# A fused attention and MLP kernel: the same instructions in newly searched orders, with the last stores planned at their traced lengths

## The chip, the cores and the metric

The kernel runs on one core of a Trainium2 chip. The metric is the device time of one execution in microseconds; lower is better. Engines are named as in the profile: PE (TensorE), DVE (VectorE), ACT (ScalarE), POOL (GpSimd) and SP (SyncE, which only issues DMAs here).

## The reference

Causal attention with 16 extra "beacon" keys that every query sees, over 8 batches x 8 heads, 576 queries and head size 64; then a gated MLP over the 4608 tokens.

```python
scores = scale * np.matmul(q, k_all.transpose(0, 1, 3, 2))   # k_all: beacon_k, then k
scores = np.where(causal, -1000000000.0, scores)
a = np.exp(scores - scores.max(-1, keepdims=True))
a /= a.sum(-1, keepdims=True) + 1e-09
attn = np.matmul(a, v_all)                                    # (8, 8, 576, 64)
x = attn.transpose(0, 2, 1, 3).reshape(4608, 512)
h = x @ w_in                                                  # (512, 2048)
g = h * (1.0 / (1.0 + np.exp(-1.702 * h)))
out = g @ w_out                                               # (2048, 512)
```

## The kernel before

**Attention.** The 64 pairs of batch and head form 16 sets of four heads. The scores of a set are made transposed, keys on the partitions, in chunks of up to 512 columns a head (`e_qk`, matmuls at L559 and L570). ACT takes the exponential (L582), POOL sets the masked part of each block to zero (`affine_select`, L600), and from the fifth set on DVE adds up the key blocks for the softmax's denominators ("zs", `e_zadd`, L618). Products with v and with ones follow (`e_av`, L658), then transposes and a reciprocal on DVE (L668 to L679), and the normalized values go to `xT` (L696).

**MLP.** The tokens are cut into ten groups: two of 256 and eight of 512. Groups 2 to 9 compute the second matmul by seven products of a Strassen-like scheme (`products`, `e_prod`, L838): DVE first forms sums of quarters of g (`e_s`, L786, called "sums" below: 128x512 elements each, four a sum), PE multiplies, and DVE joins the products into the output tiles (`e_join`, L854). The first matmul of groups 3 to 9 is partly done the same way (`fast`, L925, with sums of the weights "SF" and of the tokens "sig"), and partly plainly (L720). A store of a 256x256 quarter of the output is one DMA of 256 KB issued by SP (`e_store4`, L862).

**The last group.** Its products come as 1, 2, 6, 7, 5, 4, 3. The quarters of the output lie in tiles "a" (product 2), "b" (product 5), "u" (product 4) and "m" (product 3). Products 5 and 3 share two accumulators, one for each half of 128 rows, so that the first half of "m" is stored on its own as 128 KB and the second half in two pieces of 64 KB, one on SP and one on ACT (`e_store2`, L869).

**What sets the order.** `Plan.op` records each piece of work with an engine, a planned duration in ns and what it depends on; "Q" is a planned DMA queue that issues nothing. `Plan.run` (its body is printed below) does not choose an order: it takes each engine's list from the table `ORDER` and the PSUM bank of each accumulator from the table `BANK`. Both tables were written by a search outside the program. The planned durations settle only in which order the program's text is emitted, and so the waits are the dependences alone. DVE and POOL are planned as excluding each other for the operations named in `HELD` and for the masks. A planned duration is the search's belief, and not what the chip does: for one sum 336 ns, for a mask 190 + 0.9 ns for each element a partition.

Loads of v, q, k and the weights, and the staging copies of q and k ("qD", "kD") are DMAs that POOL issues (L458 to L502); SP issues transposing DMAs from the staged copies (L492), and stores. Each engine's list is worked off in order: an instruction that waits holds back all that stand behind it on that engine.

Of the kernel before, what the change touches and what calls it, by code (L numbers as in the profile page):

```python
# [18 lines left out]
        126, 136, 165, 162, 129, 235, 147, 150, 152, 168, 240, 171, 249, 131, 242, 174, 177, 245, 194, 200, 197,  # L19
        266, 203, 209, 206, 275, 256, 212, 215, 284, 277, 252, 254, 261, 287, 259, 280, 180, 225, 181, 226, 291,  # L20
        289, 416, 182, 187, 188, 419, 183, 189, 227, 422, 294, 296, 228, 190, 429, 304, 318, 308, 306, 322, 302,
        324, 330, 312, 316, 320, 314, 328, 332, 310, 326, 218, 342, 447, 438, 343, 219, 344, 220, 221, 450, 351,
        362, 372, 352, 345, 476, 363, 373, 353, 364, 367, 354, 374, 610, 368, 365, 375, 369, 486, 613, 441, 370,
        445, 443, 619, 491, 386, 493, 489, 638, 387, 388, 389, 503, 379, 640, 380, 381, 505, 507, 382, 525, 519,
        539, 509, 521, 523, 512, 511, 547, 527, 528, 515, 543, 531, 537, 541, 545, 535, 549, 559, 560, 561, 643,
        629, 562, 568, 584, 569, 570, 579, 580, 800, 589, 585, 581, 571, 590, 803, 582, 586, 587, 591, 652, 806,
        592, 636, 634, 632, 655, 814, 657, 659, 596, 597, 832, 598, 599, 665, 603, 604, 835, 605, 606, 669, 671,
        866, 673, 674, 667, 677, 687, 681, 697, 711, 685, 683, 707, 689, 690, 699, 703, 701, 693, 705, 709, 721,
        722, 723, 996, 823, 876, 730, 724, 731, 732, 733, 828, 999, 830, 881, 879, 826, 883, 1006, 741, 742,
        758, 746, 747, 743, 1025, 744, 751, 748, 759, 760, 1027, 749, 752, 889, 753, 754, 1030, 891, 765, 761,  # L30
        766, 767, 895, 905, 768, 893, 931, 909, 897, 907, 898, 911, 913, 914, 927, 901, 917, 929, 921, 925, 923,
        935, 933, 945, 1016, 1039, 1187, 954, 946, 947, 955, 956, 948, 965, 966, 1190, 957, 967, 968, 1019,
        1023, 1193, 1021, 1042, 1044, 1046, 1201, 970, 982, 975, 971, 976, 1219, 972, 1052, 973, 983, 977, 1222,
        978, 984, 985, 1056, 1054, 1253, 989, 990, 1061, 991, 992, 1058, 1060, 1068, 1092, 1074, 1070, 1072,
        1090, 1064, 1076, 1077, 1096, 1094, 1088, 1086, 1098, 1084, 1080, 1108, 1210, 1263, 1399, 1117, 1109,
        1110, 1111, 1118, 1119, 1120, 1217, 1402, 1215, 1266, 1268, 1270, 1213, 1409, 1128, 1133, 1134, 1129,
        1130, 1428, 1135, 1136, 1138, 1139, 1131, 1430, 1140, 1145, 1146, 1276, 1141, 1433, 1147, 1152, 1278,
        1148, 1153, 1154, 1292, 1155, 1280, 1282, 1294, 1298, 1285, 1284, 1296, 1419, 1308, 1288, 1324, 1300,
        1310, 1301, 1328, 1326, 1330, 1312, 1332, 1333, 1304, 1442, 1424, 1316, 1336, 1317, 1314, 1447, 1449,
        1422, 1426, 1445, 1320, 1357, 1348, 1349, 1455, 1471, 1350, 1358, 1351, 1459, 1457, 1473, 1385, 1461,  # L40
        1386, 1463, 1464, 1475, 1487, 1359, 1467, 1360, 1368, 1477, 1369, 1370, 1479, 1378, 1480, 1371, 1491,
        1493, 1489, 1373, 1374, 1387, 1375, 1503, 1483, 1376, 1495, 1388, 1379, 1380, 1381, 1496, 1527, 1505,
        1507, 1392, 1393, 1528, 1394, 1395, 1499, 1512, 1511, 1509, 1582, 1536, 1529, 1552, 1515, 1537, 1538,
        1584, 1598, 1530, 1586, 1553, 1600, 1602, 1539, 1620, 1590, 1554, 1547, 1548, 1549, 1550, 1555, 1606,
        1588, 1591, 1557, 1558, 1604, 1559, 1594, 1560, 1614, 1607, 1610, 1571, 1572, 1616, 1573, 1630, 1574,
        1618, 1636, 1634, 1564, 1623, 1622, 1565, 1566, 1638, 1626, 1567, 1639, 1642, 1678, 1663, 1632, 1664,
        1654, 1655, 1665, 1656, 1673, 1674, 1666, 1657, 1675, 1679, 1680, 1676, 1683, 1684, 1685, 1681, 1686,
        1687, 1691, 1692, 1693, 1697, 1694, 1698, 1701, 1702,
# [3 lines left out]
        172, 243, 175, 178, 246, 195, 198, 201, 267, 204, 207, 210, 276, 213, 216, 278, 281, 417, 420, 184, 423,  # L52
        229, 431, 191, 430, 305, 309, 303, 307, 331, 313, 317, 323, 315, 325, 329, 321, 319, 311, 333, 327, 448,
        222, 451, 477, 350, 478, 611, 614, 620, 621, 639, 504, 641, 506, 520, 508, 526, 510, 522, 524, 540, 548,
        514, 544, 516, 532, 534, 530, 518, 546, 542, 536, 538, 550, 644, 567, 801, 804, 807, 815, 816, 833, 666,
        836, 670, 672, 868, 867, 668, 682, 678, 676, 686, 684, 680, 712, 688, 698, 700, 696, 704, 692, 702, 694,
        708, 706, 710, 997, 729, 1000, 1008, 1007, 1026, 1028, 890, 1031, 892, 906, 894, 896, 910, 908, 912,
        904, 928, 920, 916, 900, 918, 932, 922, 902, 930, 924, 926, 936, 934, 1188, 953, 1191, 1194, 1203, 1202,
        1220, 1053, 1223, 1057, 1254, 1255, 1055, 1069, 1059, 1093, 1071, 1073, 1063, 1091, 1075, 1065, 1079,
        1097, 1083, 1095, 1089, 1067, 1087, 1099, 1085, 1081, 1400, 1116, 1403, 1410, 1411, 1429, 1431, 1277,  # L60
        1434, 1279, 1293, 1281, 1283, 1299, 1295, 1291, 1297, 1309, 1289, 1325, 1287, 1303, 1329, 1327, 1331,
        1311, 1307, 1313, 1335, 1305, 1339, 1315, 1337, 1319, 1321, 1456, 1472, 1323, 1460, 1458, 1356, 1462,
        1474, 1466, 1470, 1468, 1488, 1476, 1478, 1482, 1486, 1494, 1490, 1492, 1484, 1504, 1506, 1502, 1498,
        1508, 1500, 1510, 1583, 1516, 1514, 1518, 1585, 1599, 1587, 1535, 1621, 1601, 1603, 1589, 1605, 1597,
        1593, 1595, 1615, 1613, 1617, 1609, 1631, 1611, 1619, 1637, 1635, 1641, 1627, 1643, 1629, 1625, 1633,
        1645, 1662, 1706,
# [3 lines left out]
        232, 233, 127, 157, 128, 161, 130, 167, 164, 148, 149, 151, 153, 250, 263, 132, 170, 173, 264, 413, 176,  # L70
        265, 179, 196, 199, 426, 251, 202, 205, 208, 211, 257, 258, 214, 285, 253, 255, 217, 286, 260, 415, 262,
        414, 473, 288, 290, 292, 293, 427, 616, 428, 295, 297, 434, 435, 436, 495, 298, 334, 474, 338, 299, 496,
        475, 497, 437, 335, 336, 300, 346, 339, 439, 440, 337, 341, 347, 340, 301, 348, 355, 482, 618, 617, 483,
        349, 484, 485, 359, 366, 487, 488, 442, 357, 371, 376, 358, 444, 446, 356, 492, 494, 490, 499, 390, 500,
        501, 498, 502, 625, 383, 513, 529, 533, 626, 517, 552, 556, 627, 551, 555, 628, 563, 553, 554, 564, 630,
        557, 565, 558, 566, 648, 631, 573, 649, 650, 576, 651, 574, 583, 588, 575, 653, 654, 572, 637, 635, 656,
        633, 658, 660, 593, 661, 600, 662, 663, 664, 607, 675, 819, 872, 679, 713, 717, 695, 691, 873, 874, 820,
        715, 821, 822, 714, 719, 875, 718, 727, 824, 825, 725, 877, 726, 878, 829, 738, 716, 831, 882, 880, 734,
        827, 884, 736, 720, 728, 885, 1012, 735, 737, 886, 745, 750, 887, 755, 1013, 888, 1014, 769, 1035, 762,
        899, 1015, 903, 915, 919, 1036, 1037, 938, 1038, 937, 941, 939, 942, 940, 944, 1017, 943, 949, 1018,  # L80
        950, 1040, 952, 959, 951, 1041, 962, 969, 1020, 958, 1024, 1043, 1045, 960, 1047, 1022, 1048, 1049, 961,
        1050, 974, 979, 986, 1051, 1206, 993, 1207, 1062, 1208, 1259, 1078, 1082, 1066, 1260, 1261, 1100, 1104,
        1262, 1103, 1209, 1107, 1102, 1101, 1211, 1105, 1112, 1212, 1113, 1264, 1265, 1125, 1218, 1106, 1121,
        1122, 1216, 1114, 1267, 1214, 1271, 1272, 1115, 1415, 1123, 1273, 1274, 1275, 1124, 1269, 1132, 1416,
        1137, 1417, 1142, 1438, 1149, 1439, 1440, 1418, 1156, 1290, 1286, 1420, 1302, 1441, 1340, 1306, 1421,
        1334, 1443, 1338, 1444, 1341, 1425, 1345, 1318, 1448, 1423, 1450, 1446, 1322, 1427, 1451, 1343, 1344,
        1452, 1352, 1353, 1453, 1342, 1454, 1362, 1346, 1354, 1361, 1347, 1355, 1465, 1469, 1365, 1481, 1485,
        1372, 1364, 1377, 1382, 1497, 1501, 1520, 1363, 1389, 1524, 1532, 1396, 1519, 1523, 1521, 1531, 1525,
# [1471 lines left out]
```

## Time and profile before

| what | us |
| --- | --- |
| median of three runs | 323.74 |
| lowest and highest | 323.15, 324.75 |
| the profiled execution's own time | 323.49 |
| its span, first to last instruction | 321.8 |
| PE busy | 311.4 |
| DVE busy | 249.7 |
| ACT busy | 227.1 |
| POOL busy | 135.9 |

In the rows of stretches, the columns behind the stretch are its length, then for each engine the busy us and in brackets the number of instructions, then the granted PE clock, the DMA share and GB/s. A waits row reads: who waited, at which tile and line, for whom; us in total, times, longest. A timeline row has start, duration, engine, line, operation and tiles, the number of merged instructions, and in brackets the idle time before it and what ended it; "SPq" is SP issuing a DMA. A group's row has busy us and mean ns of one, then idle time before. Matmul durations contain the pipeline's depth, so those that follow each other overlap: the start of one to the start of the next is the rate.

### The profile page before, as it was taken

What the parts mean: (1) busy time and instruction counts of PE and PEld (TensorE: products, weight loads), DVE (VectorE), ACT (ScalarE), POOL (GpSimd) and SP (SyncE); (2) the same over time, 40 slices, a digit from 0 to 9 for tenths busy, and PEclk for the clock granted to TensorE, in tenths of its full rate; (3) what the DMA queues carried; (4) which work ended last, traced back from release to release, by engine and by line L of the source; (5) the groups of instructions that cost most, each with busy time, mean ns of one, the idle gap of its engine ahead of it and who ended that gap; (6) DMA issues with size and microseconds to landing.
All of it is one profiled execution on the core that took longest, in us unless ns stands there. A gap on an engine that the chain in (4) does not pass through costs nothing.

```text
span 321.8 us, 9162 instructions
## 1 busy us (share of the span) xinstructions
PE 311.4 (97%) x3899; PEld 227.7 (71%) x3899; DVE 249.7 (78%) x489; ACT 227.1 (71%) x297; POOL 135.9 (42%) x186
## 2 busy tenths in 40 slices
PE   6999999999989999999999999999999999999992
PEld 2567874545757767776787578757788888888882
DVE  4777988489899579868987796688997973966681
ACT  1678883777748887699677977997699675466710
POOL 8759658580867902583229803900650000000000
PEclk9999999999999999999999999999999999999997
DMA  7999999998799994699199995990081000300303
GB/s 120 178 203 201 138 182 186 119 195 55 74 113 152 156 89 52 92 170 189 12 139 103 201 68 111 129 154 0 7 125 48 2 3 0 115 17 2 129 4 130
DMA packets 112522, 33.49 MB, mean 104 GB/s; under 512 B 97505, under 2 KB 109921, under 8 KB 112481
## 3 DMA queue, kind: packets, MB, share of 16 engines
q0 software_dynamic: 83008, 18.55, 65.2%
q1 hardware_dynamic: 29264, 14.28, 18.5%
q8 instruction: 30, 0.49, 0.6%
q14 instruction: 12, 0.09, 0.1%
q10 hardware_dynamic: 208, 0.07, 0.1%
HBM read 37.22 MB, written 14.22 MB: 160 GB/s over the span
## 4 chain that ended last, share of the span: by engine, by line
PE 56%; ACT 1%; DVE 1%; issue 0%; DVEq 0%
PE u L838 24%; PE u L925 16%; PE u L720 6%; PE u L658 5%; PE s L559 4%; ACT E L582 1%; DVE osb L854 0%; DVE rz L679 0%; DVE g L786 0%; ACT u L935 0%; DVE xT L696 0%; DVE zt L668 0%; ACT kn L941 0%; DVE rc L674 0%; DVEq L1555 0%
## 5 line engine op out<-in xcount | busy, mean ns | idle before, releaser
L582 ACT ACTIVATE E<-s 128x2048 f16<-128x2048 f32 (+3 forms) x59 | 90.8, 1551 | 33.4 <-PE s L570 16.5
L600 POOL TENSOR_SCALAR_AFFINE_SELECT E<-E 128x512 f16<-128x512 f16 (+3 forms) x78 | 59.2, 872 | 96.3 <-ACT E L582 85.8
L838 PEld LDWEIGHTS <-g 128*128 128x128 f16 x768 | 72.9, 98 | 12.6 <-issue 1.1
L838 PE MATMUL u<-w,g 128*128 128x256 f16 x512 | 67.3, 273 | 0.0
L720 PE MATMUL u<-xT,w 128*128 128x512 f16 (+1 forms) x320 | 59.5, 337 | 0.0
L950 ACT ACTIVATE g<-u 128x512 f16<-128x512 f32 x80 | 45.3, 608 | 13.3 <-PE u L925 7.4
L854 DVE SCALAR_TENSOR_TENSOR osb<-u,osb 128x512 f32<-128x512 f32 (+2 forms) x51 | 33.2, 655 | 23.9 <-PE u L838 22.0
L720 PEld LDWEIGHTS <-w 128*128 128x128 f16 x320 | 30.5, 98 | 21.8 <-issue 0.7
L474 POOL DMA_DIRECT2D vb<-in_v_dram x32 | 35.2, 1136 | 5.0 <-PE u L658 5.0
L925 PEld LDWEIGHTS <-SF 128*128 128x128 f16 x320 | 31.0, 98 | 7.7 <-issue 0.9
L838 PE MATMUL u<-tB,g 128*128 128x256 f16 x256 | 35.2, 273 | 0.5 <-DVE g L786 0.5
L925 PE MATMUL u<-sig,SF 128*128 128x256 f16 x240 | 33.9, 273 | 0.6 <-DVE sig L786 0.2
L696 DVE TENSOR_TENSOR xT<-u,rz 128x352 f16<-128x352 f32 (+6 forms) x58 | 25.9, 478 | 7.0 <-PE u L658 6.6
L742 ACT ACTIVATE g<-u 128x512 f16<-128x512 f32 x48 | 26.6, 617 | 4.1 <-PE u L720 4.0
L658 PE MATMUL u<-E,vb 128*32 128x352 f16 (+8 forms) x928 | 28.0, 263 | 0.3 <-DVE xT L696 0.2
L786 DVE TENSOR_TENSOR g<-g 128x512 f16<-128x512 f16 x64 | 28.0, 449 | 0.3
L618 DVE TENSOR_TENSOR zs<-zs,E 128x1344 f16<-128x1344 f16 (+2 forms) x36 | 24.0, 671 | 3.6 <-POOL E L600 1.7
L935 ACT ACTIVATE u<-u 128x512 f32<-128x512 f32 x40 | 23.1, 590 | 5.0 <-PE u L925 2.9
L925 PEld LDWEIGHTS <-w 128*128 128x128 f16 x240 | 23.3, 98 | 3.1
L658 PEld LDWEIGHTS <-vb 128*32 128x32 f16 (+1 forms) x928 | 20.2, 96 | 7.4 <-issue 3.5
L925 PE MATMUL u<-xT,w 128*128 128x256 f16 x160 | 23.6, 273 | 0.0
L944 DVE TENSOR_TENSOR u<-u,qn 128x512 f32<-128x512 f32 x20 | 13.4, 692 | 7.1 <-ACT g L950 4.1
(72 smaller groups left out, 434.3 us busy)
## 6 DMA issues: line engine op xcount, KB each, us to landing
out_dram<-osb SPq DMA_DIRECT2D x35, 256.0 KB, 3.4
vb<-in_v_dram POOLq DMA_DIRECT2D x24, 128.0 KB, 6.3
kn<-in_k_dram POOLq DMA_DIRECT2D x8, 288.0 KB, 6.7
qn<-in_q_dram POOLq DMA_DIRECT2D x8, 288.0 KB, 7.0
qD<-in_q_dram POOLq DMA_DIRECT2D x8, 288.0 KB, 8.0
kD<-in_k_dram POOLq DMA_DIRECT2D x8, 288.0 KB, 7.0
w<-in_moe_w_in_dram POOLq DMA_DIRECT2D x8, 256.0 KB, 8.2
w<-in_moe_w_out_dram POOLq DMA_DIRECT2D x4, 512.0 KB, 8.9
```

Source lines behind the costliest of these rows:

```text
L474: nc.gpsimd.dma_start(out=t[0 : hi - lo, j, h0:h1, :], in_=v[b, h0:h1, lo:hi, :].rearrange("h n d -> n h d"),)
L582: nc.scalar.activation(out=Es[s][:, h0:h1, c0:c1], in_=sall[(i, p)][:, :, o : o + c1 - c0], func=AFT.Exp, scale=0.125,)
L600: nc.gpsimd.affine_select(out=blk, in_=blk, compare_op=ALU.is_ge, fill=0.0, base=off + (Nb if j == 0 else 0), pattern=[[0, Q], [1, w]], ch ...
L658: nc.tensor.matmul(u[32 * h : 32 * h + 32, a:e], lhs, src[0:kw, h, col : col + e - a], start=first, stop=last, skip_group_check=s >= EARLY ...
L696: nc.vector.tensor_tensor(out=xT[:, 2 * hs + x : 2 * hs + x + n, at : at + c1 - c0], in0=rings[("av", s, x, half)][:, 0 : n * w].rearrange ...
L720: nc.tensor.matmul(u[:, o + a - t0 : o + e - t0], w1t[:, kp, nt * P : (nt + 1) * P], xT[:, kp, a % XR : (e - 1) % XR + 1], start=(kp == 0 ...
L742: nc.scalar.activation(out=gts[g][:, n0:n1, 0:w], in_=rings[("m1", g, n0)][:, 0 : n * w].rearrange("p (n w) -> p n w", n=n), func=AFT.Gelu ...
L786: (nc.vector if eng == "DVE" else nc.gpsimd).tensor_tensor(out=out, in0=a, in1=b, op=op)
L838: nc.tensor.matmul(u[:, HM * mt : HM * (mt + 1)], lhs[:, n, mt * P : (mt + 1) * P], rhs[:, n, :], start=(n == 0 and (mt == 0 or apart) and ...
L854: nc.vector.scalar_tensor_tensor(out=osbs[(g, dst)][:, c0:c1], in0=rings[("p", g, p)][:, c0:c1], scalar=scale_of(g), in1=osbs[(g, src)][:, ...
L925: nc.tensor.matmul(u[:, HM * n : HM * (n + 1)], lhs[x][:, (2 * i + n) * P : (2 * i + n + 1) * P], rhs[:, x, :], start=fresh and n == 0 and ...
L950: nc.scalar.activation(out=gts[g][:, n : n + 2, HM * h : HM * (h + 1)], in_=rings[src][:, :].rearrange("p (n w) -> p n w", n=2), func=AFT. ...
```

## The change

All rows of `ORDER` for PE, ACT, DVE, POOL, SP and Q, and the table `BANK`, are replaced. The instructions are the same ones with the same shapes: 577 planned operations on PE, 443 on DVE, 288 on ACT, 179 on POOL and 71 on SP. By place in the list, 380 of PE's, 364 of DVE's, 158 of ACT's, 142 of POOL's and 43 of SP's stand elsewhere, the farthest 44 places off on PE, 27 on DVE, 12 on ACT, 83 on POOL and 5 on SP. The orders were searched with longer planned durations for DVE's sums than stand in the program; those in the program do not change. In the program, the last group's stores are planned as 450 ns issues followed by a queue time, as the other groups' already were, where they had been 60 ns with none; and a DMA that ACT issues has the same 300 ns planned delay as SP's. A few rows of the tables and the code:

```diff
 ORDER = {
     "PE": [
...
-        1588, 1591, 1557, 1558, 1604, 1559, 1594, 1560, 1614, 1607, 1610, 1571, 1572, 1616, 1573, 1630, 1574,
-        1618, 1636, 1634, 1564, 1623, 1622, 1565, 1566, 1638, 1626, 1567, 1639, 1642, 1678, 1663, 1632, 1664,
-        1654, 1655, 1665, 1656, 1673, 1674, 1666, 1657, 1675, 1679, 1680, 1676, 1683, 1684, 1685, 1681, 1686,
-        1687, 1691, 1692, 1693, 1697, 1694, 1698, 1701, 1702,
...
+        1618, 1616, 1564, 1634, 1565, 1566, 1567, 1639, 1638, 1622, 1654, 1623, 1642, 1626, 1655, 1632, 1663,
+        1656, 1684, 1664, 1665, 1657, 1674, 1675, 1666, 1679, 1680, 1681, 1676, 1682, 1677, 1685, 1686, 1687,
+        1688, 1693, 1694, 1695, 1696, 1700, 1701, 1705, 1706,
...
     "SP": [
...
-        1197, 963, 1251, 1249, 987, 980, 1405, 1407, 994, 1143, 1126, 1150, 1157, 1390, 1397, 1383, 1366, 1576,
-        1562, 1569, 1545, 1700, 1696, 1672, 1704, 1690,
+        1197, 1251, 1249, 963, 1407, 980, 987, 994, 1405, 1157, 1126, 1150, 1143, 1383, 1366, 1397, 1390, 1576,
+        1562, 1569, 1545, 1672, 1691, 1698, 1703, 1708,
...
     def lat(self, d, o):
         if o.eng == "Q":
-            return 300 if d.eng == "SP" else 500 if d.name[:2] == "st" else 1200
+            return 300 if d.eng in ("SP", "ACT") else 500 if d.name[:2] == "st" else 1200
...
         def store(o, i, r, c):
-            x = op("SP", 60 if g == NG - 1 else 450, [o], lambda: e_store4(g, i, r, c), name=f"store{g}")
-            ends.setdefault(g, []).append(x if g == NG - 1 else op("Q", 1200, [x], lambda: None, name=f"store{g}q"))
+            x = op("SP", 450, [o], lambda: e_store4(g, i, r, c), name=f"store{g}")
+            ends.setdefault(g, []).append(op("Q", 1200, [x], lambda: None, name=f"store{g}q"))
...
                     q = "ACT" if x else "SP"
-                    op(q, 60, [o], lambda a=a, c0=c0, c1=c1, q=q: e_store2(g, "m", 0, 1, a, c0, c1, q), name=f"store{g}")
+                    x = op(q, 450, [o], lambda a=a, c0=c0, c1=c1, q=q: e_store2(g, "m", 0, 1, a, c0, c1, q), name=f"store{g}")
+                    op("Q", 600 // parts, [x], lambda: None, name=f"store{g}q")
```

The numbers count the planned operations as the program records them, so the six new "Q" operations shift those of the last group by up to six. In SP's last five, 1700 of before is the first half of "m" (128 KB), 1696 "u", 1672 "a", 1704 SP's piece of the second half of "m" (64 KB) and 1690 "b"; after, the same stores are 1703, 1698, 1672, 1708 and 1691: a, b, u, and then the two of "m". In PE's lists of the last group, one of product 3's first-half parts stood between the last two parts of product 4; after, all parts of product 4 come ahead of product 3's. On DVE, the last sum 1 of group 2 (named 1 as the second of the four sums) comes ahead of the two 1.26 us transposes of set 7 instead of behind them.

181 rows, old and new, of tables (BANK, ORDER) are left out of this document.

## The prediction

> **What bounds the kernel now.** I read the page first, then the waits of TensorE, the stretches of the span, and last the timeline at two places: the costliest stall and the end.
>
> ```profile
> PE 311.4 (97%) x3899; PEld 227.7 (71%) x3899; DVE 249.7 (78%) x489; ACT 227.1 (71%) x297; POOL 135.9 (42%) x186
> ...
> 140.00:160.00 20.00, 19.79 (x253) 13.30 (x254) 17.50 (x33) 17.97 (x26) 8.40 (x10) 1.00 1.00 121
> ...
> 310.00:322.00 12.00, 6.00 (x55) 5.13 (x53) 4.15 (x10) 0.00 (x0) 0.00 (x0) 0.85 0.26 87
> ```
>
> TensorE (PE) is the bound: 311.4 of 321.8 us busy, at the full clock (the column behind the five engines is the granted clock, 1.00 in the stretch shown). No instruction is added or removed, so the change can take only from the 10.4 us in which PE is idle and from what a "busy" PE loses to short waits. Of the 10.4 us, 6.0 lie at the end (310:322 has 12 us and 6.00 busy) and 2.6 at the start. The other 1.8 us are in the waits, of which the start's and four of seven more are:
>
> ```profile
> PE u L1523 <- DVE tB L369: 2.6, 1, 2.6
> PE u L838 <- DVE g L786: 0.5, 1, 0.5
> ...
> PE u L925 <- DVE sig L786: 0.2, 1, 0.2
> PE u L658 <- DVE osb L854: 0.2, 1, 0.2
> ...
> PE u L658 <- DVE xT L696: 0.2, 1, 0.2
> ```
>
> The first row is the start, whose orders stay: the first 39 of PE's 577 planned operations are the same. The seven others are one wait each, from 0.5 down to 0.2 us. Each is larger than it shows, because the end of the matmul before it overlaps the wait. At the largest one:
>
> ```profile
> 88.27 0.60 PE L838 MATMUL u<-tB,sA 128*128 128x256 f16 x4
> 88.80 0.64 PE L570 MATMUL s<-qT,kT 32*128 32x320 f16 x16
> 89.37 0.61 PE L838 MATMUL u<-w,g 128*128 128x256 f16 x4
> 90.43 0.39 PE L838 MATMUL u<-tB,g 128*128 128x256 f16 x2 [0.45 <-DVE g L786]
> ...
> 314.09 0.60 PE L838 MATMUL u<-tB,g 128*128 128x256 f16 x4
> 314.53 1.47 PE L838 MATMUL u<-w,g 128*128 128x256 f16 x12
> ```
>
> Four such matmuls take 0.44 us from start to start (314.09 to 314.53). At 89.37 the next four start 1.06 us later, so 0.62 us are lost where 0.45 is shown as idle: 0.17 more. Seven stalls then lose about 1.8 + 7 x 0.17 = 3.0 us, all that a better order in the middle can win.
>
> **Term 1, the last group's stores.** The rows of the end:
>
> ```profile
> 314.73 1.02 DVE L854 SCALAR_TENSOR_TENSOR osb<-u,osb 128x512 f32<-128x512 f32 x2 [1.37 <-PE u L838]
> 315.77 0.34 SPq L869 DMA_DIRECT2D out_dram<-osb  x1
> 316.04 0.49 DVE L854 SCALAR_TENSOR_TENSOR osb<-u,osb 128x128 f32<-128x128 f32 x2 [0.29 <-PE u L838]
> 316.16 0.97 SPq L862 DMA_DIRECT2D out_dram<-osb  x2
> 316.56 0.43 ACTq L869 DMA_DIRECT2D out_dram<-osb  x1
> 317.24 0.44 SPq L869 DMA_DIRECT2D out_dram<-osb  x1
> 317.72 0.68 SPq L862 DMA_DIRECT2D out_dram<-osb  x1
> ...
> SPq L869 <- DVE osb L854: 11.6, 1, 11.6
> ...
> DMA to landing us min/median/max: 2.2/2.8/3.7
> ...
> DMA to landing us min/median/max: 1.8/2.2/2.4
> ```
>
> PE is done at 314.53 + 1.47 = 316.00 and the last joins at 316.53, but the last store is issued at 317.72. It is a 256 KB store of tile "b", whose joins were done long before the join at 314.73. In SP's list of before, the 128 KB store (315.77) stands ahead of three 256 KB stores ("u", "a", "b"), so SP waits 11.6 us for one join and then issues five stores in a row. The landing rows are those of L862 (256 KB) and of L869 (128 and 64 KB): 317.72 + 2.8 = 320.5, and the span ends 1.3 us behind that.
>
> After the change SP's list is a, b, u, then the 128 KB store, then its 64 KB store, and the other 64 KB stay on ACT; VectorE makes ACT's piece first in both. "a" and "b" leave while PE still works. Product 4 (into "u") is finished before the shared bank's last four parts, where in before one of these stood ahead of its end; so its join can begin 0.44 us earlier, at 314.29 instead of 314.73, and ends before 315.3 even with the 1.02 us of both joins of that row. "u" is issued by 315.3, the 128 KB store by 315.8 as today, and SP's last one when its join ends, 316.53, at 316.56. That is the time of ACT's row today, which waited for the same join. It lands 2.2 us later, at 318.8, against 320.5: **-1.7 us**. With 1.8 and 2.4 us of landing it is -2.1 and -1.5. Do the bytes allow it?
>
> ```profile
> 317.00:318.00 1.00, 0.00 (x0) 0.00 (x0) 0.00 (x0) 0.00 (x0) 0.00 (x0) 1.00 0.90 296
> ...
> 319.00:320.00 1.00, 0.00 (x0) 0.00 (x0) 0.00 (x0) 0.00 (x0) 0.00 (x0) 0.50 0.87 310
> 320.00:321.00 1.00, 0.00 (x0) 0.00 (x0) 0.00 (x0) 0.00 (x0) 0.00 (x0) 0.50 0.00 1
> ```
>
> The six stores, 1 MB in all, take until 320.0 at about 300 GB/s, so they began near 316.6: today's end is bound by bytes. After the change 512 KB remain from 315.3 on, 1.7 us at that rate; begun 0.9 us after their first issue (315.77 to some 316.6 today) they are through at 317.9, before the 64 KB store's landing. So latency bounds, not bytes. SP then waits for the lanes' semaphores one behind the other; with an earlier lane landing last, up to 0.4 us could change, which I leave out of the value and inside the range.
>
> **Term 2, changes of tile shape on PE.** A group of 64- or 32-row score products between 128-row ones costs about 0.09 us at its entry: 0.53 from 88.27 to 88.80 against 0.44. Counted in the two orders, changes between score products, attention-value products and the rest fall from 135 to 132: 3 x 0.1 = **-0.3 us**, or nothing if the others take longer.
>
> **Term 3, the VectorE sums.** Why did PE wait at 90.43?
>
> ```profile
> 87.71 1.26 DVE L525 STREAM_TRANSPOSE kT<-kn 128x576 f32<-128x576 f32 x1
> 88.81 0.85 DVE L618 TENSOR_TENSOR zs<-zs,E 128x1344 f16<-128x1344 f16 x1
> 89.57 0.80 DVE L786 TENSOR_TENSOR g<-sA,g 128x512 f16<-128x512 f16 x1
> ...
> 89.03 2.27 POOL L600 TENSOR_SCALAR_AFFINE_SELECT E<-E 128x448 f16<-128x448 f16 x1
> 90.05 1.91 POOL L474 DMA_DIRECT2D vb<-in_v_dram  x1
> ...
> 306.24 0.42 DVE L786 TENSOR_TENSOR g<-sA,g 128x512 f16<-128x512 f16 x1
> ```
>
> The sum that PE needed took 0.80 us beside a mask on GpSimd; alone (306.24, where GpSimd is idle) the same form takes 0.42. And it stood behind two transposes (the second at 87.71) and a 0.85 us sum of zs. In the new order this sum (group 2, sum 1, last quarter) comes ahead of all three, 2 x 1.26 + 0.85 = 3.4 us of VectorE work earlier, and its reader is still the last part of product 6: that stall goes, 0.62 us. The next one (0.2 shown, at the attention-value product behind it, for a join that frees its bank) gets another product part ahead of it and other banks: about 0.3 us. The wait of L925 for "sig" keeps as much VectorE work ahead of it, and at the first tiles of group 4 PE's order is the same as before, so I leave these. Value: **-0.9 us**. Bounds: all seven stalls gone, -3.0; on the other side, the sums could meet masks at other places.
>
> ```profile
> L786 DVE TENSOR_TENSOR g<-g 128x512 f16<-128x512 f16 x64 | 28.0, 449 | 0.3
> L786 DVE TENSOR_TENSOR g<-sA,g 128x512 f16<-128x512 f16 x32 | 14.3, 450 | 2.2 <-PE u L838 1.7
> ...
> L786 DVE TENSOR_TENSOR sig<-xT 128x512 f16<-128x512 f16 x14 | 7.7, 551 | 0.0
> L786 DVE TENSOR_TENSOR sig<-xT,sig 128x512 f16<-128x512 f16 x14 | 6.9, 495 | 0.2
> L600 POOL TENSOR_SCALAR_AFFINE_SELECT E<-E 128x512 f16<-128x512 f16 x42 | 36.1, 918 | 57.3 <-ACT E L582 55.3 <-issue 2.0
> L488 POOL DMA_DIRECT2D qD<-in_q_dram x8 | 16.3, 2035 | 0.0
> L474 POOL DMA_DIRECT2D vb<-in_v_dram x32 | 35.2, 1136 | 5.0 <-PE u L658 5.0
> ```
>
> Against 0.42 alone these 124 sums are stretched by 64 x 0.03 + 32 x 0.03 + 14 x 0.13 + 14 x 0.075 = 5.8 us in all, of which PE pays 3.0 at most. Twice the stretch would cost another 3.0 if all of it came through; the other VectorE work hides two thirds of it today if PE's shown 1.8 us are what comes through, so I take two thirds of the 3.0, +2.0, as the upper end.
>
> The Trainium skill (SBUF — State Buffer, "Who interferes with whom") says that VectorE with two SBUF inputs and a GpSimd instruction that reads SBUF take turns: the second is fully blocked until the first ends. The trace agrees if GpSimd is timed by its starts: mask at 89.03, next at 90.05, and the sum ends 0.32 us behind that. By that rule the stretch depends only on which sum starts behind which mask, so a new order can trade one blocked sum for another; I take this up as a rival.
>
> **What moves at no cost.** Transposing DMAs on SP now stand behind other stores of group 2; their readers come over 10 us later, and GpSimd's loads and staging come in another order, covered by its idle time (58% of the span). If SP's cover were gone, a transposing DMA would be late by its store's wait; GpSimd's is priced below. ScalarE's order follows its producers. The new planner delay for ACT's DMA acts only through the order.
>
> **Sum.** -1.7 - 0.3 - 0.9 = -2.9 us on the profiled execution's 323.49 us (span 321.8, 1.7 around it): **320.6 us**. That execution lies 0.25 us below the median of the three runs, 323.74, and inside their spread.
>
> **Rivals.** (a) The stalls only move: terms 1 and 2 alone, 323.49 - 2.0 = 321.5. For it: the program's own durations of the sums are not changed, and VectorE is busy for 78% of the span, so what moves forward pushes something back. Against it: the first stall's sum really moves. (b) All stalls go: 323.49 - 2.0 - 3.0 = 318.5. Against it: group 4's start is the same. (c) Sums are blocked elsewhere: two more wait out a mask of 0.92 us in place of the two stalls removed, -0.9 + 1.8 = +0.9 in place of term 3: 323.49 - 2.0 + 0.9 = 322.4. (d) The end is hidden anyway: one of the last stores takes the 3.7 us of the longest landing above, and ends near 320.3 again: terms 2 and 3 alone, 323.49 - 1.2 = 322.3. Against it: 512 KB fewer are in its way. That the change does not do what it says is (a). (e) **Slower**: GpSimd becomes late. In the new order two loads of v and two staging DMAs stand between the masks of set 8 and the first mask of set 9: 2 x 1.14 + 2 x 2.04 = 6.4 us at most, where two loads and one staging DMA stood, 4.3. If the exponentials wait for that whole block, the mask is 6.4 us late, the sums of set 9 and the attention-value product behind them too, and PE, which works in order, stands: 321.5 + 6.4 = 327.9. It decides from 3.9 us of lateness on. Against it: GpSimd is busy 8.40 of 20 us in 140:160, so 11.6 us are there to hide the block, which needs no exponential to begin.
>
> **How the numbers follow.** Chances: forecast 0.50, (a) 0.22, (b) 0.08, (c) 0.08, (d) 0.05, (e) 0.07. Half a per cent, about what a measurement can tell from no change, is 1.6 us: faster is below 322.1, slower above 325.4. Faster: 0.50 + 0.22 + 0.08 = 0.80; same: 0.08 + 0.05 = 0.13; slower 0.07. The bounds of the three terms give 323.49 - 2.1 - 0.3 - 3.0 = 318.1 and 323.49 - 1.5 + 2.0 = 324.0; the range that leaves out half of (b), (e) and the outermost ends is 318.7 to 323.0.
>
> **What would show it.** Right: the last store issued within 0.1 us of the last join, PE's end to the span's end shrinking from 5.8 to about 4.0 us; no wait of L838 for a sum near 90 us; PE's end near 314.8. Wrong: a new large wait of PE for VectorE or GpSimd before 240 us, or a last landing still 4 us after PE's end.

## The result and the profile after

The kernel after takes 320.63 us (median), the one before 323.59 us beside it: a ratio of 0.9898 with a 95% interval of 0.9864 to 0.9932. One of the four executions of after took 396.49 us at a mean granted clock of 0.757; the ratio leaves it out, and the median without it is 320.54 us. The profiled execution took 320.54 us with a span of 318.8 us. First the page of after and its TensorE waits:

```profile
span 318.8 us, 9159 instructions
PE 309.6 (97%) x3899; PEld 227.4 (71%) x3899; DVE 247.4 (78%) x489; ACT 226.8 (71%) x297; POOL 137.3 (43%) x186
...
PE p L570 <- DVE qT L525: 0.9, 1, 0.9
PE u L925 <- ACT g L950: 0.7, 1, 0.7
PE u L925 <- DVE sig L786: 0.4, 1, 0.4
```

TensorE is still the bound. The wait of L838 for a VectorE sum is gone, and a new one, 0.7 us for ScalarE at L950, has come. The first row lies in the first 20 us, among the warm-up matmuls; PE reaches the attention-value product behind them at 20.30 us (20.31 before), so it costs nothing. The end, in the timeline and in the row of L869's DMAs, after:

```profile
313.35 1.91 PE L838 MATMUL u<-w,g 128*128 128x256 f16 x16
314.87 1.28 SPq L869 DMA_DIRECT2D out_dram<-osb  x2
315.29 0.49 DVE L854 SCALAR_TENSOR_TENSOR osb<-u,osb 128x128 f32<-128x128 f32 x2 [0.45 <-PE u L838]
315.62 0.38 ACTq L869 DMA_DIRECT2D out_dram<-osb  x1
...
L869 SPq DMA_DIRECT2D out_dram<-osb x2: 344/344/345, 314.9 to 315.8; - x2
...
DMA to landing us min/median/max: 1.7/1.7/1.9
```

PE ends at 313.35 + 1.91 = 315.26, 0.74 us earlier than before. The last join ends at 315.78 and the last store is issued at 315.8, at once. From PE's end to the span's end it is 318.8 - 315.26 = 3.5 us, where it was 5.8. So of the 3.0 us that the span lost, **2.3 lie behind PE's last matmul and 0.7 ahead of it**. Where do the 0.7 come from? The stretches of the span between the start and the end, before and then after; the first column behind the length is PE's busy time:

```profile
85.00:110.00 25.00, 23.91 (x381) 17.61 (x380) 21.40 (x34) 18.12 (x20) 19.97 (x24) 1.00 1.37 124
...
128.00:145.00 17.00, 16.54 (x245) 12.12 (x244) 13.40 (x25) 14.20 (x15) 11.94 (x15) 1.00 1.10 127
145.00:235.00 90.00, 89.81 (x1113) 65.44 (x1112) 74.83 (x145) 72.30 (x90) 38.83 (x48) 1.00 0.94 100
235.00:250.00 15.00, 15.00 (x174) 12.53 (x173) 12.33 (x21) 14.13 (x25) 4.67 (x7) 1.00 0.45 85
```
```profile
85.00:110.00 25.00, 24.75 (x390) 18.68 (x389) 21.45 (x36) 18.47 (x21) 17.89 (x20) 1.00 1.43 127
...
128.00:145.00 17.00, 16.18 (x221) 11.62 (x210) 13.39 (x25) 14.07 (x18) 12.84 (x15) 1.00 1.51 140
145.00:235.00 90.00, 90.00 (x1127) 65.80 (x1126) 71.55 (x143) 72.11 (x90) 36.37 (x46) 1.00 0.79 92
235.00:250.00 15.00, 14.21 (x145) 11.87 (x144) 12.37 (x19) 13.90 (x24) 3.66 (x5) 1.00 0.23 72
```

PE's idle time falls from 1.09 to 0.25 us in 85:110 and from 0.19 to nothing in 145:235. It rises from 0.46 to 0.82 in 128:145 and from nothing to 0.79 in 235:250. Gained 1.03, given back 1.15: in shown idle time the new orders won nothing. That hides most of it, because the end of a matmul overlaps the wait behind it. The starts tell more. Where PE has done the same matmuls in both kernels, counted by tiles and shape, the next one can be compared; here with 3059 and with 3175 of them done, each time before and then after:

```profile
235.35 0.62 PE L559 MATMUL s<-qT,kT 64*128 64x224 f16 x12
233.80 0.62 PE L559 MATMUL s<-qT,kT 64*128 64x224 f16 x12
```
```profile
246.48 1.47 PE L925 MATMUL u<-sig,SF 128*128 128x256 f16 x12
245.97 1.48 PE L925 MATMUL u<-sig,SF 128*128 128x256 f16 x12
```

At 83 us after is 0.09 us behind. At 104 us it is 1.43 ahead and at 235 us 1.55, so most of it is won between 83 and 104 us, around the old stall. **Around the new stall at 241 us, 1.05 of it is lost again**; 0.50 is left at 246 us and 0.74 at PE's end. The new stall, in the timeline of after (VectorE, GpSimd, ScalarE, TensorE):

```profile
238.71 1.97 DVE L618 TENSOR_TENSOR zs<-zs,E 128x832 f16<-128x832 f16 x1
240.61 0.69 DVE L944 TENSOR_TENSOR u<-u,qn 128x512 f32<-128x512 f32 x1
...
237.69 2.54 POOL L600 TENSOR_SCALAR_AFFINE_SELECT E<-E 128x320 f16<-128x320 f16 x3
...
241.33 1.08 ACT L950 ACTIVATE g<-u 128x512 f16<-128x512 f32 x2 [0.91 <-DVE u L944]
...
241.13 0.60 PE L925 MATMUL u<-xT,w 128*128 128x256 f16 x4
242.46 0.60 PE L925 MATMUL u<-xT,w 128*128 128x256 f16 x4 [0.73 <-ACT g L950]
```

Read from the bottom: PE waits for a bank that ScalarE frees, ScalarE waits for VectorE's sum at L944, and that one stands behind a sum of zs which takes 1.97 us while GpSimd works through three masks.

### The profile page after: what moved, and what is told of

It is laid out like the page before. It is cut to its first block, busy times and chain, and to the rows that moved or that the text cites. A ratio compares the mean times of both kernels' runs of the same rounds, so it can differ in the third digit from the quotient of the medians.

```text
span 318.8 us, 9159 instructions
## 1 busy us (share of the span) xinstructions
PE 309.6 (97%) x3899; PEld 227.4 (71%) x3899; DVE 247.4 (78%) x489; ACT 226.8 (71%) x297; POOL 137.3 (43%) x186
## 4 chain that ended last, share of the span: by engine, by line
PE 91%; DVE 3%; DMA 2%; ACT 2%; issue 1%; POOL 0%; DVEq 0%; ACTq 0%; POOLq 0%
PE u L838 31%; PE u L720 18%; PE u L925 17%; PE u L658 10%; PE u L766 4%; PE s L559 4%; PE s L570 4%; DMA qn<-in_q_dram 2%; PE u L1524 2%; PE p L570 1%; ACT E L582 1%; DVE osb L854 1%; DVE sig L786 1%; DVE zs L618 1%; DVE qT L525 0%
## 5 line engine op out<-in xcount | busy, mean ns | idle before, releaser
L600 POOL TENSOR_SCALAR_AFFINE_SELECT E<-E 128x512 f16<-128x512 f16 (+3 forms) x78 | 57.6, 771 | 96.1 <-ACT E L582 81.3
L838 PEld LDWEIGHTS <-g 128*128 128x128 f16 x768 | 73.4, 98 | 11.8 <-issue 1.3
L838 PE MATMUL u<-w,g 128*128 128x256 f16 x512 | 68.0, 273 | 0.0
L950 ACT ACTIVATE g<-u 128x512 f16<-128x512 f32 x80 | 44.7, 612 | 18.5 <-DVE u L944 9.3
L854 DVE SCALAR_TENSOR_TENSOR osb<-u,osb 128x512 f32<-128x512 f32 (+2 forms) x51 | 33.2, 655 | 19.9 <-PE u L838 18.9
L838 PE MATMUL u<-tB,g 128*128 128x256 f16 x256 | 34.7, 273 | 0.0
L474 POOL DMA_DIRECT2D vb<-in_v_dram x32 | 32.6, 1055 | 1.7 <-PE u L658 1.6
L618 DVE TENSOR_TENSOR zs<-zs,E 128x1344 f16<-128x1344 f16 (+2 forms) x36 | 23.7, 675 | 5.0 <-POOL E L600 4.5
L658 PE MATMUL u<-E,vb 128*32 128x352 f16 (+8 forms) x928 | 27.2, 263 | 0.2 <-DVE osb L854 0.2
L786 DVE TENSOR_TENSOR g<-g 128x512 f16<-128x512 f16 x64 | 26.4, 431 | 0.3
L944 DVE TENSOR_TENSOR u<-u,kn 128x512 f32<-128x512 f32 x20 | 13.1, 694 | 10.6 <-PE u L925 6.1
```

The costliest lines, as they stand in the source:

```text
L474: nc.gpsimd.dma_start(out=t[0 : hi - lo, j, h0:h1, :], in_=v[b, h0:h1, lo:hi, :].rearrange("h n d -> n h d"),)
L600: nc.gpsimd.affine_select(out=blk, in_=blk, compare_op=ALU.is_ge, fill=0.0, base=off + (Nb if j == 0 else 0), pattern=[[0, Q], [1, w]], ch ...
L618: nc.vector.tensor_tensor(out=t, in0=E[:, :, Z0:S] if i == 1 else t, in1=E[:, :, wcol[i] : wcol[i] + S - a], op=ALU.add,)
L658: nc.tensor.matmul(u[32 * h : 32 * h + 32, a:e], lhs, src[0:kw, h, col : col + e - a], start=first, stop=last, skip_group_check=s >= EARLY ...
L786: (nc.vector if eng == "DVE" else nc.gpsimd).tensor_tensor(out=out, in0=a, in1=b, op=op)
L838: nc.tensor.matmul(u[:, HM * mt : HM * (mt + 1)], lhs[:, n, mt * P : (mt + 1) * P], rhs[:, n, :], start=(n == 0 and (mt == 0 or apart) and ...
```

## Experiments

Each was run beside the kernel before on the same chip. The kernel before had medians of 323.54, 323.19, 323.38 and 323.70 us in the four groups of runs. PE's order is the same in all of them up to the attention-value product at 20.3 us, yet the profiled executions reach it between 19.64 and 20.49 us. So PE's time is also given from that product to its last matmul: 295.69 us before and 294.96 after.

**The end alone, put in and taken out.** First the kernel before with the last five stores in the new order, then the kernel after with the old one.

```diff
-        1562, 1569, 1545, 1700, 1696, 1672, 1704, 1690,
+        1562, 1569, 1545, 1672, 1690, 1696, 1700, 1704,
```

> The kernel before with only SP's last five stores in the order a, b, u, m, m. Theory (the end is worth about two thirds of the gain, whatever the middle does): 323.6 - 2.0 = 321.6 us, PE's last matmul still ending near 316.0, the span's end 3.5 to 4.0 us behind it. Rival (the gain comes from the orders in the middle, and the end is bound by something else): not below 323.0 us.

```diff
-        1562, 1569, 1545, 1672, 1691, 1698, 1703, 1708,
+        1562, 1569, 1545, 1703, 1698, 1672, 1708, 1691,
```

> The kernel after with SP's last five stores in the old order (first m, u, a, second m, b). Theory (the end alone): 320.6 + 2.0 = 322.6 us, PE's last matmul still near 315.3, the last store issued over 1 us behind the last join. Rival (the middle): within 0.5 us of 320.6.

Measured: 321.74 us (ratio to before 0.9936, 0.9916 to 0.9955) and 322.23 us (0.9955, 0.9940 to 0.9969). The list of SP alone gives 1.8 us in the old kernel, and taking it out of the new one costs 1.6 us. PE's time from the product at 20.3 us is 295.70 and 294.92 us, as in the kernels that they were made from: the end and the middle are separate gains. In the second, the timeline shows the old picture again, the last 256 KB store well behind the last join (314.98 + 0.49):

```profile
314.56 0.34 SPq L869 DMA_DIRECT2D out_dram<-osb  x1
314.96 0.96 SPq L862 DMA_DIRECT2D out_dram<-osb  x2
314.98 0.49 DVE L854 SCALAR_TENSOR_TENSOR osb<-u,osb 128x128 f32<-128x128 f32 x2 [0.45 <-PE u L838]
315.31 0.45 ACTq L869 DMA_DIRECT2D out_dram<-osb  x1
316.02 0.44 SPq L869 DMA_DIRECT2D out_dram<-osb  x1
316.50 0.67 SPq L862 DMA_DIRECT2D out_dram<-osb  x1
```

**Is the moved sum what takes the stall at 90 us away?** In the kernel before, on VectorE, the sum s (349) ahead of the two transposes (618, 617) and the second zs sum (483):

```diff
-        482, 618, 617, 483, 349, 484, 485, 359, 366,
+        482, 349, 618, 617, 483, 484, 485, 359, 366,
```

> The kernel before with one move on DVE: the last sum 1 of group 2 comes ahead of set 7's two transposes and the second zs sum. Theory (a stall taken away on PE comes through to its end): no wait of PE for a sum near 90 us, PE's last matmul 0.5 to 0.6 us earlier, near 315.4, time 323.0. Rival (given back at the next waits): the wait at 90 us is gone, but PE's end stays within 0.2 us of 316.0 and the time within 0.2 us of 323.6.

Measured: 323.94 us, ratio 1.0009 (0.9997 to 1.0022). The theory fell. The wait for the sum is gone, and a longer one stands at the next product; PE's time from the product at 20.3 us grew to 296.25 us, a loss that the rival did not allow either:

```profile
90.83 0.60 PE L838 MATMUL u<-w,g 128*128 128x256 f16 x4
92.55 0.38 PE L658 MATMUL u<-zs,ones 128*32 128x288 f16 x8 [1.11 <-DVE osb L854]
```

That names a join, so in the next run the join (359) moved ahead of the zs sums as well:

```diff
-        482, 618, 617, 483, 349, 484, 485, 359, 366,
+        482, 349, 618, 617, 359, 483, 484, 485, 366,
```

> The kernel before with the sum of group 2 moved ahead as in the earlier run, and the first of the two joins behind the zs sums moved ahead of the last three zs sums as well. Theory (in that run PE waited 1.1 us for the bank that this join frees): the wait is under 0.4 us, PE's end at least 0.4 us earlier than before's, time 322.9 to 323.2. Rival (the attention-value product there needs the zs sums at that time anyway): a wait of at least 0.8 us stays and the time is 323.6 or more.

Measured: 323.89 us, ratio 1.0019 (1.0006 to 1.0032): the rival. The same product now waits for the zs sums:

```profile
PE u L658 <- DVE zs L618: 1.0, 1, 1.0
```

The third try kept the moved sum and gave PE other work ahead of that product (486): the next chunk of scores (613) and a part of product 7 (370).

```diff
-        368, 365, 375, 369, 486, 613, 441, 370, 445,
+        368, 365, 375, 369, 613, 370, 486, 441, 445,
```

> The kernel before with the sum of group 2 moved ahead on DVE, and on PE the denominators' product of set 5 two pieces later (behind the next chunk of scores and a part of product 7, 0.56 + 0.44 us). Theory (what takes the stall away in the kernel after is PE's order: more other work stands ahead of the product that needs the zs sums): the 1.18 us lost there with the sum alone moved fall under 0.3, PE's end comes near 315.4 and the time to 322.8 to 323.1 us. Rival (the product and its norms are then late for what follows): a new loss of 0.5 us or more behind it and not below 323.5 us.

Measured: 325.33 us, ratio 1.0049 (1.0029 to 1.0069), from 323.32 to 327.0 from run to run. Slower, as the rival had it: in the profiled execution PE loses time at this product, at the next ones and for the norms behind them, and then the granted clock falls (second fence; the stretches are 2 us long):

```profile
92.97 0.38 PE L658 MATMUL u<-zs,ones 128*32 128x288 f16 x8 [0.74 <-DVE osb L854]
...
93.75 1.14 PE L658 MATMUL u<-E,vb 128*32 128x224 f16 x36 [0.35 <-DVE osb L854]
95.77 1.30 PE L658 MATMUL u<-E,vb 128*32 128x352 f16 x20 [0.88 <-DVE xT L696]
```
```profile
92.00:94.00 2.00, 0.91 (x28) 0.63 (x29) 1.91 (x4) 1.61 (x1) 0.23 (x1) 1.00 1.92 129
94.00:96.00 2.00, 1.12 (x40) 0.77 (x31) 1.93 (x6) 0.00 (x0) 0.00 (x0) 0.88 1.66 107
96.00:98.00 2.00, 2.00 (x56) 1.39 (x52) 1.97 (x5) 0.00 (x0) 0.00 (x0) 0.50 0.01 1
```

VectorE is busy for 1.83 to 1.97 of each 2 us from 90 to 98 us, and these moves on it only changed who waited. The last run does not show what PE's order is worth in the old orders: in its profiled execution the moved sum itself took 1.84 us beside the masks, where it had taken 0.85 us in the two runs before. Then the same two parts were undone, one at a time, in the kernel after.

```diff
-        348, 349, 356, 482, 617, 618, 483, 359, 358,
+        348, 356, 482, 617, 618, 483, 349, 359, 358,
```

> The kernel after with the sum of group 2 that it moved ahead put back behind set 7's two transposes and the second zs sum. Theory (within the new orders that move is what takes the stall near 90 us away): its reader waits 0.8 to 1.1 us near 90 us, and the time is 321.3 to 321.7. Rival (the new orders have room for it): within 0.2 us of 320.6.

```diff
-        365, 372, 373, 374, 613, 375, 486, 441,
+        365, 372, 486, 373, 374, 613, 375, 441,
```

> The kernel after with the denominators' product of set 5 four pieces earlier on PE (ahead of two parts of product 5, the next chunk of scores and another part, 3 x 0.44 + 0.56 us), much as the kernel before had it. Theory (the new PE order covers the VectorE work that this product needs): PE waits 1.5 to 2 us there for the zs sums, and the time is 321.8 to 322.5. Rival (the pieces behind it fill in): within 0.3 us of 320.6.

Measured: 321.21 us (0.9923, 0.9908 to 0.9938) and 322.29 us (0.9952, 0.9936 to 0.9968), against 320.63 for the kernel after. The waits that came back, of the first and of the second:

```profile
90.96 0.61 PE L838 MATMUL u<-tB,g 128*128 128x256 f16 x4 [0.71 <-DVE g L786]
```
```profile
91.77 0.38 PE L658 MATMUL u<-zs,ones 128*32 128x288 f16 x8 [1.62 <-DVE zs L618]
```

So in the new orders both parts are needed, and PE's own order is the larger one: four pieces, 3 x 0.44 + 0.56 = 1.9 us of other matmuls, stand ahead of the product that needs the zs sums. In the old orders the sum alone did not help, nor did the sum with two pieces; four pieces, or PE's part alone, were not tried there. The two medians are 0.6 and 1.7 us above that of the kernel after; they come from another group of runs, so these differences carry the spread of both, and the first one's interval overlaps that of after. PE's time from the product at 20.3 us, free of the scatter of the start, is 296.16 and 296.65 us against 294.96.

**The new stall at 241 us.** One swap on VectorE in the kernel after, ScalarE's next sum (1290) ahead of the long zs sum (1417):

```diff
-        1142, 1149, 1124, 1438, 1417, 1290, 1156,
+        1142, 1149, 1124, 1438, 1290, 1417, 1156,
```

> The kernel after with one swap on DVE: the sum 21 of group 7's first tile comes ahead of the third zs sum of set 14, which took 1.97 us beside the masks. Theory (PE's new 0.9 us stall at 241 us comes from that blocked zs sum, by way of ScalarE): the stall shrinks to under 0.3 us and the time to about 319.9 us. Rival (ScalarE is late by itself behind its table load): the stall stays over 0.6 us and the time within 0.2 us of 320.6.

Measured: 319.48 us, ratio 0.9865 (0.9842 to 0.9888): **faster than both kernels**, 1.1 us below the kernel after. The two intervals overlap (0.9864 to 0.9932 for after), but its four executions lie from 319.06 to 319.59 and three of after from 320.14 to 320.72, beside nearly the same median of the kernel before (323.54 and 323.59). PE's time from the product at 20.3 us falls from 294.96 to 294.20 us; the rest of the profiled pair's 0.95 us is nearly all an earlier start. The zs sum now starts behind the masks and is short, and PE runs through:

```profile
239.52 0.70 DVE L944 TENSOR_TENSOR u<-u,qn 128x512 f32<-128x512 f32 x1 [0.87 <-PE u L925]
240.13 0.58 DVE L618 TENSOR_TENSOR zs<-zs,E 128x832 f16<-128x832 f16 x1
...
241.00 1.04 PE L925 MATMUL u<-xT,w 128*128 128x256 f16 x8
```

Another such step on top of that swap, at PE's loss at 136 us, put the four token sums of group 4 ahead of the join before them:

```diff
-        574, 600, 661, 662, 663, 664, 607,
+        574, 661, 662, 663, 664, 600, 607,
```

> The kernel of the swap at 241 us, with the four token sums of group 4 (sig) ahead of the join that stands in front of them on DVE. Theory (PE's 0.55 us loss at 136 us is those sums being late, one join's 0.6 us late): that loss falls under 0.15 us and the time by 0.4 to 0.5 us, to 319.0. Rival (the join is then late for the bank it frees, as the moved sum showed): another wait takes its place and the time stays within 0.2 us of 319.5 or rises.

Measured: 320.59 us, 0.9911 (0.9898 to 0.9924): the rival, 1.1 us worse than without it. ScalarE then waits for that join's bank, and PE for ScalarE:

```profile
135.97 0.58 ACT L935 ACTIVATE u<-u 128x512 f32<-128x512 f32 x1 [2.15 <-DVE osb L854]
...
136.60 1.03 PE L925 MATMUL u<-sig,SF 128*128 128x256 f16 x8 [0.88 <-ACT u L935]
```

**Are the long sums waiting for the masks?** In `e_mask` of the kernel after GpSimd's part is left out, once for the sets 14 and 15 and once from the fifth set on; the condition stands in the first line of the function.

```diff
+        if s >= 14:
+            return
         w = e - a
```

> The kernel after, with GpSimd's masks of the sets 14 and 15 left out (later queries of the last batch also see later keys). Theory (the 1.97 us zs sum at 239 us waited for those masks): it takes 0.59 us, PE's 0.9 us stall there falls under 0.3, and the time is 319.5 to 320.0 us. Rival (it is long for a reason of its own): 1.97 us stay and so does the stall.

> The kernel after, with GpSimd's masks left out from the fifth set on (queries of those sets also see later keys). Theory (masks lengthen DVE's sums, and through them PE waits): all 124 sums of g and sig mean 0.42 us, the losses at 136 and 241 us are gone, 318.9 to 319.6 us. Rival (PE's waits come from the orders and from ScalarE, and the masks only stretch what nobody waits for): 320.3 to 320.7 us.

The first took 319.26 us (0.9876, 0.9860 to 0.9892), a little less than the theory's range; its zs sum takes 0.58 us and PE's stalls near 240 us are gone:

```profile
238.08 0.58 DVE L620 TENSOR_TENSOR zs<-zs,E 128x832 f16<-128x832 f16 x1
```

The second (condition `s >= EARLY`) took 321.12 us (0.9924, 0.9903 to 0.9945), longer than the theory and the rival allowed. The lengths came out as expected: groups by shape, first of after, then without the masks, where the two new lines shift L618 and L786 by two.

```profile
L618 DVE TENSOR_TENSOR zs<-zs,E 128x832 f16<-128x832 f16 x12 | 8.8, 743 | 0.0
L786 DVE TENSOR_TENSOR sig<-xT,sig 128x512 f16<-128x512 f16 x14 | 7.1, 507 | 0.3
```
```profile
L620 DVE TENSOR_TENSOR zs<-zs,E 128x832 f16<-128x832 f16 x12 | 6.8, 584 | 0.8 <-ACT E L582 0.8
L788 DVE TENSOR_TENSOR sig<-xT,sig 128x512 f16<-128x512 f16 x14 | 5.9, 421 | 0.3
```

The 0.55 us loss at 136 us and the 0.9 us loss at 241 us are gone too. Up to 200 us PE gains 1.2 us on the kernel after, counted from the product at 20.3 us. What the time lost again in the profiled execution, the longest of the four (319.78 to 321.69 us), is one wait of PE for a transposing DMA, and the clock behind it. By the starts of the same matmuls it cost 2.6 us, and the slow clock 1.5 us more:

```profile
203.46 1.03 PE L559 MATMUL s<-qT,kT 64*128 64x256 f16 x12 [2.53 <-DMA kT<-kD]
...
204.00:206.00 2.00, 2.00 (x18) 1.45 (x15) 0.00 (x0) 1.46 (x2) 0.00 (x0) 0.50 2.43 155
```

Why that DMA landed late without the masks was not tried.

## Why the prediction was right, and where not

The time came out at 320.63 us where 320.6 was forecast, and faster as forecast. By its terms it is less exact: in the profiled pair the end gave 0.6 us more than its 1.7 and the middle 0.5 us less than its 1.2. These errors cancelled, so that the sum fits to 0.1 us is luck.

- **What bounds.** TensorE before and after: right.
- **Term 1, the end, -1.7 us.** The mechanism was right and shown from both sides: -1.8 us put in, +1.6 us taken out. Counted from PE's end to the span's end, both experiments have 2.0 us and the pair of before and after 2.3. Too long was the landing: the prediction took 2.2 us, the median of three stores in the crowded end of before; after, SP's last store takes 1.7. Issue at 315.8 plus 1.7 plus the same 1.3 us to the span's end gives the 318.8. That latency and not bytes bounds the new end fits: the stretches of after behind PE's end (the last two columns are the DMA engines' busy share and GB/s) show next to nothing moving from 317 us on.

```profile
316.00:317.00 1.00, 0.00 (x0) 0.00 (x0) 0.00 (x0) 0.00 (x0) 0.00 (x0) 1.00 0.73 241
317.00:318.00 1.00, 0.00 (x0) 0.00 (x0) 0.00 (x0) 0.00 (x0) 0.00 (x0) 1.00 0.02 4
```

- **Term 2, -0.3 us.** No run separates it. It stays inside what PE won by 235 us.
- **Term 3, -0.9 us.** Its two stalls went, as forecast, though a wait of 0.25 us for a join (L854) stands behind them at 93.45 us. With term 2, PE had won 1.55 us by 235 us, more than the 1.2 of both terms. The sum had no term for the new stall at 241 us; around it 1.05 us were lost again, and 0.74 us reached PE's end. And the step "that stall goes", argued from the one sum's move, was wrong as an argument: that move alone made nothing faster in the old orders. The product behind it needs the zs sums and a join from the same busy VectorE, and the new PE order covers them. The prediction had weighed PE's order as a small matter ("another product part ahead of it").
- **Rivals.** (c), sums blocked behind masks elsewhere, happened in part: 1.97 us in place of 0.58 for one zs sum, 0.9 us on PE, and undoing it took 1.1 us off the time. It was forecast with two sums of group size and not with one of zs, and its full time did not come: one sum was blocked, and the 1.55 us were already won. Part of (a) is the same event, a stall that moved from 90 to 241 us, but (a) put all of term 3 at nothing. (b), (d) and (e) did not happen; GpSimd's longer block ahead of set 9 left no wait of PE in 145:235.
- **VectorE and GpSimd taking turns.** The Trainium skill's rule (SBUF — State Buffer, "Who interferes with whom") that the second of the two engines is blocked until the first ends agrees with these traces: the same zs sum takes 1.97 us beside three masks, 0.58 behind them, and 0.58 with the masks left out.

## What to carry to other kernels

Look at the issue queue of the last stores before anything else: one store that waits at the head of a queue held back three that were ready before it, and five numbers in a list were worth 1.8 of 3 us. Around 90 us, where VectorE was over 90% busy, moving one or two of its instructions only changed who waited; the cover came from the order of the engine that waits. At 241 us one swap on VectorE did pay, because it also took a sum out from among the masks (1.97 us became 0.58). So an instruction that another engine can block should not stand ahead of one that a chain waits for: that swap took 1.1 us off the searched orders. And judge an order by the starts of the same matmuls, not by shown idle time alone.

## What the runs showed of the hardware that was not expected

TensorE's clock can fall in the middle of a run through a stall of a few us. Without the masks, a wait of 2.53 us was followed by a granted clock of 0.50 in 204:206, and in the run with PE's order moved, 4 us in which PE was busy for 0.91 and 1.12 of 2 us each were followed by 0.50 in 96:98, though no single wait there was over 0.9 us. So the price of a long stall can be more than its length: the first cost 2.6 us, and 1.5 us more behind it.

The Trainium skill (TensorE: Matmul & The Clock Gate, Part 1) has the clock halve after an idle window of about 3.4 us; in neither of these two cases was PE without matmuls for that long at a stretch, and the clock fell all the same.
